# Batch 0 by halves of the heads, banks 4 and 5 as one tile, and batch 2's first matmul plain, in a fused cosformer attention and MLP kernel

## The chip, the cores and the metric

The kernel runs on one core of one Trainium2 chip. The metric is the time of one execution in microseconds (us) as the device takes it; times given as a median are over several executions of the same program. A profile comes from one execution of its own, which has its own time.

## The reference

The input is q, k and v of shape (8 batches, 8 heads, 576 positions, 64 features) and two weights, w_in (512 x 2048) and w_out (2048 x 512), all float32. First a linear attention with cosine weights, then an MLP with a squared ReLU:

```python
def phi(x, c, s):
    r = np.maximum(x, 0.0)
    return np.concatenate([r * c, r * s], axis=-1)
q_p, k_p = phi(q, cos_w, sin_w), phi(k, cos_w, sin_w)
kv = np.einsum('bhsf,bhsd->bhfd', k_p, v)
z = np.sum(k_p, axis=2)
num = np.einsum('bhsf,bhfd->bhsd', q_p, kv)
den = np.einsum('bhsf,bhf->bhs', q_p, z)[..., None] + 1e-06
x = (num / den).transpose(0, 2, 1, 3).reshape(4608, 512)
r = np.maximum(x @ w_in, 0.0)
out = (r * r) @ w_out
```

Each of the 4,608 tokens (8 batches of 576) is a row of x with 8 heads of 64 features.

## The kernel before, in words

**Tiles.** A batch's 576 positions are four tiles of 128 (called j = 0 to 3) and a tail of 64 rows; the tails of two batches share one tile. The MLP takes the 512 main tokens of batch b as group m = b, and the eight tails, 512 tokens together, as a ninth group m = 8. TensorE works on bf16 copies.

**Attention of a batch.** ScalarE (ACT) and VectorE (DVE) make the features of k and q, 128 x 512 at a time: relu times cosine and relu times sine (`feat`, L341 on ACT, L345 on DVE). v is cast into `vext`, which has a column of ones beside each head (L363, L365; for batch 0 by halves of the heads, `first_v`, L398), so that the product kv also yields z. TensorE makes kv for each head (`att_kv`, L387; batch 0: `first_kv`, L412, into bank 4 for heads 0 to 3 and bank 5 for heads 4 to 7), and a copy takes it to SBUF (`att_kvz`, L458; `first_kvz`, L423). q's features are transposed on TensorE in batches 0 and 1 (L480, copy L488), by DMA in the later ones. `att_num` (L499; `first_num`, L430) makes numerator and denominator, `att_div` (L517, L520, L523; `first_div`, L442, L443, L445) the reciprocal and the division on DVE. x is transposed (L545, copy L549; later by DMA) into xT for the MLP.

**First matmul of the MLP (x @ w_in, relu, square).** In batch 0 it runs in steps `first_mm(s, a, ...)` (L712), each on four of the sixteen hidden blocks of 128 columns and half of the tokens (256), with `first_relu` on ACT (L722) and `first_square` on DVE (L731); s goes through FIRST_S, eight steps. In batch 1 it is plain: `unit_mm` (L584) has four matmuls of 512 columns per hidden block (the first three blocks by halves, `unit_half`, L568), then a relu on ACT (L593) and squares on DVE (L601). From batch FIRST_7 = 2 on it is a scheme with seven products of half-sized blocks instead of eight (`plan_gemm1_7`; `in_product`, L661, 256 columns each), which has 112 matmuls of 256 columns per group in place of 64 of 512, but sums of x (L643), of w_in (L619, four sums, once), copies between banks on ACT (L1060, L1077), additions (L684) and maxima (L693) on DVE besides.

**Second matmul (g @ w_out).** Batch 0: `first_out` (L737) into banks 4, 5, 0, 1, with copies L770. Batch 1: plain, `out_pair` (L751) into banks 4 and 5, with copies L761. Later groups: seven products again (`plan_gemm2`; `product`, L850), with X = bank 4 and Y = bank 5 as accumulators, sums of w_out and of g on DVE (L810, L829), a copy between the banks on ACT (L1142), a copy of the fifth product's result to SBUF (L1165), and the results read by ACT (L1152) or added on DVE (L1148) into ysb, from which SP stores them (L776). In the last group (m = 8) other banks are used and the stores are split over queues: `put_part` (L784) and `put_quarter` (L792).

**PSUM.** Six banks of 128 x 512 float32, each a tile of its own (bank 0 to 5), and abank, a tile of two banks, for kv and num of the attention.

**Loads.** SP issues k, k's tail, q's tiles 0 and 1, v's first half, v's tail, v's second half and q's tiles 2 and 3 of batch 0, and later most loads and stores. POOL's queue carries w_in in four quarters, then q of batch 1 (L218), a quarter of w_out (L301), k and its tail, a quarter, v and its tail of batch 1, and two quarters. A small POOL copy ahead of these (`gate`) reads batch 0's v, first half, and so holds them until it has landed.

**What sets the order.** All of it, from the warm-up matmuls of TensorE (38 on zeros, L369) to the last store, is written down as operations with an engine (or a choice of ACT and DVE), an assumed duration, the keys they read and write, and due times; the table SHIFTS moves the due time of single operations, by their number. `Plan.order` starts, engine by engine, the ready operation that is due first, and the operations are then issued in the order of these planned starts. On the chip each engine takes its instructions strictly in that order and waits by semaphores for the tiles that it touches. Planned times (`given` for the landing of loads, `pool` for POOL's queue, `hold` for the loads of batch 2) only affect the order. The waits are made by tile: two accesses to the same tile are ordered if they may overlap.

The function that writes the list, in its part for batch 0's first matmul:

```python
for a in range(2):
    to = 2 * (n % 2) + a
    add("PE", 8 * 0.1092 * step / W, lambda a=a, c0=c0: first_mm(s, a, c0, step),
        r=[("xT", 0, j) for j in js] + [("w1", hq)], w=[("bank", to)], due=...)
```

Of the kernel before, what the change touches and what calls it, by code (L numbers as in the profile page):

```python
# [158 lines left out]
def kernel(  # L159
# [330 lines left out]
    NUM = [abank[:, 0, :], abank[:, 1, :]]  # L490

    def att_num(b, j, num=NUM):
# [13 lines left out]

    def att_div(b, j, num=NUM):
        n = 2
        if num is NUM:
            parts = [(0, n, abank[:, 0:n, 0 : HH * E1])]  # L510
        else:
            parts = [(i, i + 1, num[i][:, 0 : HH * E1].unsqueeze(1)) for i in range(n)]
        parts = [(a, z, t.rearrange("p b (h e) -> p b h e", e=E1)) for a, z, t in parts]
        den = odd.tile([P, 2, HH], F32, name="den", tag="den", bufs=2)
        rden = odd.tile([P, 2, HH], F32, name="rden", tag="rden", bufs=2)
        for a, z, n4 in parts:
            nc.vector.tensor_single_scalar(  # L517
                out=den[:, a:z], in_=n4[:, :, :, D], scalar=EPS, op=ALU.add
            )
        nc.vector.reciprocal(out=rden[:, 0:n], in_=den[:, 0:n])  # L520
        x = x_of(b, j).rearrange("p (b k) (l d) -> p b k l d", b=n, l=2)
        for a, z, n4 in parts:
            nc.vector.tensor_tensor(  # L523
                out=x[:, a:z],
                in0=n4[:, :, :, 0:D].rearrange("p b (k l) d -> p b k l d", l=2),
                in1=rden[:, a:z]
                .rearrange("p b (k l) -> p b k l", l=2)
                .unsqueeze(4)
                .to_broadcast([P, z - a, HH // 2, 2, D]),
                op=ALU.mult,  # L530
            )
# [10 lines left out]
    def att_x_pe(b, j, to):  # L542
        dst = as_bf16(bank[to][:, :], KB)
        for kb in range(KB):
            nc.tensor.transpose(dst[:, kb, :], x_of(b, j)[:, kb, :], ident[:, :])  # L545

# [157 lines left out]
    FIRST_S = (0, 4, 1, 5, 2, 6, 3, 7)  # L704

    def first_mm(s, a, c0, step):
        half, hq = s // 4, s % 4
        for c in (c0,):
            for i in (2 * a, 2 * a + 1):
                hb = hq * 4 + i  # L710
                for kb in range(KB):
                    nc.tensor.matmul(  # L712
                        out=bank[2 * (FIRST_S.index(s) % 2) + i // 2][:, i % 2 * W + c : i % 2 * W + c + step],
                        lhsT=w1sb[:, kb, hb * P : (hb + 1) * P],
                        rhs=xT_of(0)[:, half, kb, c : c + step],
                        start=(kb == 0),
                        stop=(kb == KB - 1),
                    )
# [229 lines left out]
    def plan_qT(b, i):  # L948
# [3 lines left out]
        for j in js:  # L952
            where[b, j] = ("qpT", i)
# [4 lines left out]
    def plan_qT_pe(b, j, to, due, eng):  # L958
# [3 lines left out]
        add(eng, cost(eng, 1024, "psum") if eng == "ACT" else 0.60, lambda: att_qT_copy(b, j, 0, H, to, ENG[eng]),  # L962
            r=[("bank", to)], w=[("qpTp", slot)])
        where[b, j] = ("qpTp", slot)
# [4 lines left out]
    def plan_num(b, j, due):  # L969
        r = [where[b, j], ("kvz", b % 3)] + ([("kvz", (b + 1) % 3)] if j == J else [])  # L970
        add("PE", 0.27 if j < J else 0.36, lambda: att_num(b, j), r=r, w=[("T",)], due=due)
# [489 lines left out]
```

## Time and profile before

| what | value |
|---|---|
| median of three runs | 275.63 us (275.6 to 275.7) |
| the profiled execution | 276.42 us |
| its span (first to last instruction) | 274.6 us |
| granted clock of TensorE, mean | 0.996 |
| TensorE (PE) busy | 265.0 us, 96% |
| VectorE (DVE) busy | 225.9 us, 82% |
| ScalarE (ACT) busy | 186.8 us, 68% |
| GpSimd (POOL) busy | 15.2 us, 6% |
| read from HBM, written | 36.70 MB, 9.44 MB |
| costliest lines on TensorE | L661 (first matmul by seven products), L850 (second) |

The page of the profile gives busy times by engine (PEld is the loading of weights, beside PE), and groups of equal instructions by line, "out<-in" by the program's names, with the idle time of the engine just before them and what ended it. The chain of waits starts at the last instruction and goes back, at each step, to what released it, or to the instruction before it on its engine; "PE bank L661" is work of TensorE on line 661, "DMA k<-in_k_dram" a load, "issue" time without a wait that the profile shows. The windows give busy times for stretches of the span; a DMA share above 1 means that the packets' times overlap on the 16 DMA engines. Lines of the timeline are runs of one instruction, with start, length, and in brackets the idle time before them and what ended it. SPq, ACTq and POOLq are the engines' issue of DMAs.

### The profile page before, as it was taken

The page shows a single profiled execution, that of the slowest core. Times are in us where ns is not written, and L with a number is a line of the kernel's source. Part 1 is how long each engine was busy: PE and PEld are TensorE (multiplying, and loading weights), DVE is VectorE, ACT ScalarE, POOL GpSimd, SP SyncE. Part 2 cuts the span into 40 slices and gives each one's busy share as a digit, 9 for nine tenths or more (in the row PEclk, how much of TensorE's full clock was granted, in tenths as well). Part 3 has the DMA queues.
Part 4 walks back from the last instruction along what each step waited for, and adds up shares of the span by engine and source line. Part 5 has one row for each costly group of instructions (what it writes and reads, how often), then busy time and mean ns, then how long its engine had stood idle before and what let it go on. Part 6 is the DMA issues. An engine that isn't in the chain of part 4 may idle for free.

```text
span 274.6 us, 6700 instructions
## 1 busy us (share of the span) xinstructions
PE 265.0 (96%) x2698; PEld 215.2 (78%) x2706; DVE 225.9 (82%) x450; ACT 186.8 (68%) x336; POOL 15.2 (6%) x29
## 2 busy tenths in 40 slices
PE   8989999999999999999999999999999999999993
PEld 3669856565478669899998889989988888888882
DVE  1865997947969999999999999999989974888911
ACT  3865671696689899898879997865646763464231
POOL 1563100000000000000000000000000000000022
PEclk9999999999999999999999999999999999999998
DMA  7999999999998979999999999985202100300134
GB/s 213 306 204 276 284 279 284 296 245 297 264 289 255 259 202 282 329 246 168 287 301 241 230 271 253 165 183 181 41 1 96 79 2 0 155 1 2 76 117 115
DMA packets 87006, 53.38 MB, mean 194 GB/s; under 512 B 56928, under 2 KB 83936, under 8 KB 86976
## 3 DMA queue, kind: packets, MB, share of 16 engines
q1 hardware_dynamic: 81504, 44.64, 63.4%
q0 software_dynamic: 5392, 8.26, 13.9%
q8 instruction: 21, 0.34, 0.5%
q10 hardware_dynamic: 80, 0.07, 0.1%
q14 instruction: 9, 0.07, 0.1%
HBM read 36.70 MB, written 9.44 MB: 168 GB/s over the span
## 4 chain that ended last, share of the span: by engine, by line
PE 80%; DMA 8%; DVE 3%; SPq 2%; issue 1%; ACT 1%; POOL 1%; POOLq 0%; DVEq 0%
PE bank L661 31%; PE bank L850 31%; DMA k<-in_k_dram 6%; PE bank L751 4%; PE bank L737 3%; PE abank L387 3%; PE bank L584 3%; PE abank L499 3%; DMA q<-in_q_dram 2%; DVE qp L345 1%; SPq L239 1%; ACT kp L341 1%; PE bank L568 1%; DVE gT L601 1%; SPq L249 1%
## 5 line engine op out<-in xcount | busy, mean ns | idle before, releaser
L661 PEld LDWEIGHTS <-w1sb 128*128 128x128 bf16 x448 | 43.3, 98 | 6.0
L661 PE MATMUL bank<-xT,w1sb 128*128 128x256 bf16 x336 | 47.8, 273 | 0.0
L850 PEld LDWEIGHTS <-gT 128*128 128x128 bf16 x448 | 43.3, 98 | 5.6 <-issue 0.6
L677 ACT ACTIVATE gT<-bank 128x512 bf16<-128x512 f32 x56 | 33.1, 600 | 16.9 <-PE bank L661 15.6
L850 PE MATMUL bank<-w2sb,gT 128*128 128x256 bf16 x336 | 41.9, 273 | 0.6 <-ACT ysb L761 0.6
L684 DVE TENSOR_TENSOR gT<-bank,qpTp 128x512 bf16<-128x512 f32 x56 | 36.7, 686 | 4.7 <-PE bank L661 3.7
L601 DVE TENSOR_TENSOR gT<-gT 128x2048 bf16<-128x2048 bf16 (+1 forms) x32 | 37.7, 1189 | 1.8 <-ACT gT L677 1.5
L1060 ACT COPY bank<-bank 128x512 f32<-128x512 f32 x56 | 31.4, 581 | 7.5 <-PE bank L661 7.0
L850 PEld LDWEIGHTS <-gs 128*128 128x128 bf16 x336 | 32.5, 98 | 3.8
L661 PEld LDWEIGHTS <-w1t 128*128 128x128 bf16 x336 | 31.9, 98 | 4.4
L661 PE MATMUL bank<-qpTp,w1t 128*128 128x256 bf16 x224 | 32.7, 273 | 0.0
L850 PE MATMUL bank<-w2t,gs 128*128 128x256 bf16 x224 | 27.6, 273 | 0.0
L1077 ACT COPY qpTp<-bank 128x512 f32<-128x512 f32 x28 | 16.1, 589 | 9.8 <-PE bank L661 5.6
L523 DVE TENSOR_TENSOR x<-abank,rden 128x512 bf16<-128x512 f32 x30 | 20.7, 691 | 1.0
L1148 DVE TENSOR_TENSOR ysb<-bank,y 128x512 f32<-128x512 f32 x14 | 9.7, 690 | 9.6 <-PE bank L850 8.3
L661 PE MATMUL bank<-xT,w1t 128*128 128x256 bf16 x112 | 16.8, 272 | 0.0
L661 PE MATMUL bank<-zeros,w1sb 128*128 128x256 bf16 x112 | 16.6, 273 | 0.0
L712 PE MATMUL bank<-xT,w1sb 128*128 128x256 bf16 (+1 forms) x160 | 15.5, 251 | 0.6 <-ACT gT L722 0.6
L341 ACT ACTIVATE qp<-q,sin_col 128x512 bf16<-128x512 f32 x23 | 16.1, 717 | 0.0
L784 POOL DMA_DIRECT2D out_dram<-ysb x4 | 2.4, 613 | 237.6 <-ACT ysb L1152 235.2
L341 ACT ACTIVATE kp<-k,cos_col 128x512 bf16<-128x512 f32 x18 | 12.6, 715 | 4.3 <-DMA k<-in_k_dram 4.3
L751 PE MATMUL bank<-w2sb,gT 128*128 128x512 bf16 x60 | 14.9, 379 | 0.5 <-DVE gT L601 0.3
(118 smaller groups left out, 423.5 us busy)
## 6 DMA issues: line engine op xcount, KB each, us to landing
out_dram<-ysb SPq DMA_DIRECT2D x16, 512.0 KB, 3.9
q<-in_q_dram SPq DMA_DIRECT2D x14, 512.0 KB, 6.3
v<-in_v_dram SPq DMA_DIRECT2D x14, 512.0 KB, 6.0
k<-in_k_dram SPq DMA_DIRECT2D x12, 512.0 KB, 6.7
w1sb<-in_moe_w_in_dram POOLq DMA_DIRECT2D x4, 512.0 KB, 9.3
w2sb<-in_moe_w_out_dram POOLq DMA_DIRECT2D x4, 512.0 KB, 17.5
k<-in_k_dram SPq DMA_DIRECT2D x1, 1024.0 KB, 5.6
q<-in_q_dram POOLq DMA_DIRECT2D x1, 1024.0 KB, 11.9
```

The lines of the kernel that those rows point to most:

```text
L341: eng.activation(out=dst[ps, :, lo : lo + D], in_=src[ps], func=ACTF.Relu, scale=col[ps])
L523: nc.vector.tensor_tensor(out=x[:, a:z], in0=n4[:, :, :, 0:D].rearrange("p b (k l) d -> p b k l d", l=2), in1=rden[:, a:z] .rearrange("p b ...
L601: nc.vector.tensor_tensor(out=g, in0=g, in1=g, op=ALU.mult)
L661: nc.tensor.matmul(out=bank[to][:, s * W : (s + 1) * W], lhsT=lhs[:, kb, (2 * u + s) * P : (2 * u + s + 1) * P], rhs=rhs[:, kb, :], start= ...
L677: nc.scalar.activation(out=g_pair(m, i, j, u), in_=bank[to][:, :].rearrange("p (s c) -> p s c", s=2), func=ACTF.Relu,)
L684: nc.vector.tensor_tensor(out=g_pair(m, i, j, u), in0=bank[to][:, :].rearrange("p (s c) -> p s c", s=2), in1=in_five(u).rearrange("p (s c) ...
L712: nc.tensor.matmul(out=bank[2 * (FIRST_S.index(s) % 2) + i // 2][:, i % 2 * W + c : i % 2 * W + c + step], lhsT=w1sb[:, kb, hb * P : (hb + ...
L751: nc.tensor.matmul(out=bank[LAST_Y[s_]][:, :], lhsT=gT_of(m)[:, hb, tt * P : (tt + 1) * P], rhs=w2sb[:, hb, :], start=(hb == 0), stop=(hb ...
L850: nc.tensor.matmul(out=bank[to][:, s * DM2 : (s + 1) * DM2], lhsT=lhs[:, hb, s * P : (s + 1) * P], rhs=rhs[:, hb, :], start=(fresh and hb ...
L1060: add("ACT", psum, lambda: nc.scalar.copy(out=bank[b][:, :], in_=bank[a][:, :]), r=[("bank", a)], w=[("bank", b)])
L1077: add("ACT", psum, lambda u=u, Y=Y: nc.scalar.copy(out=in_five(u), in_=bank[Y][:, :]), r=[("bank", Y)], w=five)
L1148: lambda: nc.vector.tensor_tensor(out=y_view(m, i, cc), in0=half_bank(a), in1=five_of(m)[:, :, :], op=ALU.add),
```

## The change

- **PSUM.** Banks 4 and 5 become the halves of one tile of two banks, `bbank`; "bank 6" is a name for abank's first half.
- **Batch 0's loads.** k's and v's tails are issued by ScalarE's queue, ahead of its own table load and activations; SP keeps k, q's tiles 0 and 1, v's halves, q's tiles 2 and 3, in this order. The gate on POOL reads v's tail instead of v's first half.
- **Batch 0's attention.** The copies of q's transposes go by halves of the heads (`att_qT_part`), on whichever of ACT and DVE is planned first; x of tiles 0 and 1 is transposed and copied by halves of the heads, all into bank 4 (`first_x_pe`, `first_x_copy`); kv takes tiles (0, 1), (2, 3) and the tail as separate steps. Both q transposes of tiles 2 and 3 use bank 5. num of tile 3 is written to bbank, and x's transposes of tiles 2 and 3 to bank 6 and bank 4.
- **Batch 0's first matmul.** Step s = 0 is split once more, by halves of the inner dimension (`kbs`), each needing only the x of one half of the heads. FIRST_S keeps four steps (hidden blocks 0 to 7); blocks 8 to 15 become plain units of 512 columns (`unit_mm`) with squares by four blocks.
- **Batch 2.** FIRST_7 goes from 2 to 3: batch 2's first matmul is plain, its sums, additions, maxima and copies between banks go, and the four sums of w_in move to batch 3.
- **att_div** loses its form for separate banks. The planned times of loads and the holds of batch 2's loads change, and SHIFTS is replaced by a new table throughout (cut here).

```diff
-    bank = [psum.tile([P, FP], F32, name=f"bank{i}") for i in range(6)]
+    bank = [psum.tile([P, FP], F32, name=f"bank{i}") for i in range(4)]
+    bbank = psum.tile([P, 2, FP], F32, name="bbank")
     abank = psum.tile([P, 2, FP], F32, name="abank")
+    bank += [bbank[:, 0, :], bbank[:, 1, :], abank[:, 0, :]]
...
-        nc.gpsimd.tensor_copy(out=got[:, :], in_=kqv["v", 0][:, 0, 0, 0:1])
+        nc.gpsimd.tensor_copy(out=got[rows(0), :], in_=kqv["vt", 0][rows(0), 0, 0:1])
...
+    def att_qT_part(b, j, h0, h1, to, eng):
...
+        copy(out=qpTs[b, j, "t"][:, h0:h1, :], in_=as_bf16(bank[to][:, :], H)[:, h0:h1, :])
...
+    def first_x_pe(j, half, to):
+        dst = as_bf16(bank[to][:, :], 2 * KB)
+        for kb in (2 * half, 2 * half + 1):
+            nc.tensor.transpose(dst[:, KB * j + kb, :], x_of(0, j)[:, kb, :], ident[:, :])
+
+    def first_x_copy(j, half, to, eng):
+        copy = eng.copy if eng is nc.scalar else eng.tensor_copy
+        kbs = slice(2 * half, 2 * half + 2)
+        copy(
+            out=xT_of(0)[:, j // 2, kbs, j % 2 * P : (j % 2 + 1) * P],
+            in_=as_bf16(bank[to][:, :], 2 * KB)[:, KB * j + 2 * half : KB * j + 2 * half + 2, :],
+        )
...
-    FIRST_S = (0, 4, 1, 5, 2, 6, 3, 7)
-
-    def first_mm(s, a, c0, step):
+    FIRST_S = (0, 4, 1, 5)
+
+    def first_mm(s, a, c, step, kbs=range(4)):
...
+        for k0 in range(2 if s == 0 else 1):
+            kbs = (2 * k0, 2 * k0 + 1) if s == 0 else range(KB)
+            for c0, step in parts:
...
         for js, r in (
-            (range(J), [("v0", half, i) for i in range(2)] + [("kp", j, x) for j in range(J) for x in "cs"]),
+            ((0, 1), [("v0", half, 0)] + [("kp", j, x) for j in (0, 1) for x in "cs"]),
+            ((2, 3), [("v0", half, 1)] + [("kp", j, x) for j in (2, 3) for x in "cs"]),
             ((J,), [("kpt", 0, "c"), ("kpt", 0, "s"), ("vt", 0, 0)]),
         ):
...
-        plan_num(0, j, TM + 0.5 + 0.8 * (j - 2))
-        plan_x_pe(0, j, 4 + j % 2, TM + 1.8 + 0.8 * (j - 2), "DVE")
+        keys = [("T",), ("bank", 4), ("bank", 5)][j - 2 :][: j - 1]
+        plan_num(0, j, TM + 0.5 + 0.8 * (j - 2), (abank, bbank)[j - 2], keys)
+        plan_x_pe(0, j, (6, 4)[j - 2], TM + 1.8 + 0.8 * (j - 2), None, keys)
...
+    for hb in range(4 * len(FIRST_S) // 2, HB):
+        n = hb - 4 * len(FIRST_S) // 2
+        plan_unit(0, hb, n % 4, TM + len(FIRST_S) * dt0 + n * dt0 / 2)
...
-    FIRST_7, STRIDE, SHIFT = 2, 2.0, -6.0
+    FIRST_7, STRIDE, SHIFT = 3, 2.0, -6.0
...
-            hold = {"v": 41.0, "k": 43.0, "q": 43.1}[nm] if b == 2 else 0.0
+            hold = {"v": 40.0, "k": 41.5, "q": 41.6}[nm] if b == 2 else 0.0
...
         load_main("k", 0, nc.sync)
-        load_tail("k", 0, nc.sync)
+        load_tail("k", 0, nc.scalar)
+        load_tail("v", 0, nc.scalar)
         load_tiles("q", 0, nc.sync, slice(0, 2))
         load_half("v", 0, nc.sync, 0)
-        load_tail("v", 0, nc.sync)
         load_half("v", 0, nc.sync, 1)
         load_tiles("q", 0, nc.sync, slice(2, 4))
```

More of the change, by code (lines that the diff above doesn't have):

```diff
@@ L505, in att_num, with att_div @@
                     )
[L507 to L513, printed above, removed]
+    def att_div(b, j, to=abank):
+        n4 = to[:, :, 0 : HH * E1].rearrange("p b (h e) -> p b h e", e=E1)
         den = odd.tile([P, 2, HH], F32, name="den", tag="den", bufs=2)
         rden = odd.tile([P, 2, HH], F32, name="rden", tag="rden", bufs=2)
[L516 to L531, printed above, removed]
+        nc.vector.tensor_single_scalar(out=den[:, :], in_=n4[:, :, :, D], scalar=EPS, op=ALU.add)
+        nc.vector.reciprocal(out=rden[:, :], in_=den[:, :])
+        x = x_of(b, j).rearrange("p (b k) (l d) -> p b k l d", b=2, l=2)
+        nc.vector.tensor_tensor(
+            out=x[:, :],
+            in0=n4[:, :, :, 0:D].rearrange("p b (k l) d -> p b k l d", l=2),
+            in1=rden[:, :]
+            .rearrange("p b (k l) -> p b k l", l=2)
+            .unsqueeze(4)
+            .to_broadcast([P, 2, HH // 2, 2, D]),
+            op=ALU.mult,
+        )
     def att_x(b, i):
@@ L701, in in_max @@
         nc.vector.tensor_single_scalar(out=g, in_=g, scalar=0.0, op=ALU.max)
-    FIRST_S = (0, 4, 1, 5, 2, 6, 3, 7)
-    def first_mm(s, a, c0, step):
+    FIRST_S = (0, 4, 1, 5)
+    def first_mm(s, a, c, step, kbs=range(4)):
         half, hq = s // 4, s % 4
[L708 to L718, printed above, removed]
+        for i in range(2):
+            hb = hq * 4 + 2 * a + i
+            for kb in kbs:
+                nc.tensor.matmul(
+                    out=bank[2 * (FIRST_S.index(s) % 2) + a][:, i * W + c : i * W + c + step],
+                    lhsT=w1sb[:, kb, hb * P : (hb + 1) * P],
+                    rhs=xT_of(0)[:, half, kb, c : c + step],
+                    start=(kb == 0 and i == 0 and c == 0),
+                    stop=(kb == KB - 1),
+                    skip_group_check=True,
+                )
     def first_relu(s, a):
@@ L961, in plan_qT_pe, with plan_num @@
         add("PE", 8 * 0.057, lambda: att_qT_pe(b, j, 0, H, to), r=q_parts((j,)), w=[("bank", to)], due=due)
-        add(eng, cost(eng, 1024, "psum") if eng == "ACT" else 0.60, lambda: att_qT_copy(b, j, 0, H, to, ENG[eng]),
-            r=[("bank", to)], w=[("qpTp", slot)])
-        where[b, j] = ("qpTp", slot)
+        if b == 0:
+            for h in (0, HH):
+                add(EITHER, (0.33, 0.48), lambda e, h=h: att_qT_part(b, j, h, h + HH, to, ENG[e]),
+                    r=[("bank", to)], w=[("qpTp", slot, h)])
+            where[b, j] = [("qpTp", slot, 0), ("qpTp", slot, HH)]
+        else:
+            add(eng, cost(eng, 1024, "psum") if eng == "ACT" else 0.60, lambda: att_qT_copy(b, j, 0, H, to, ENG[eng]),
+                r=[("bank", to)], w=[("qpTp", slot), ("qpTp", slot, 0), ("qpTp", slot, HH)])
+            where[b, j] = [("qpTp", slot)]
     def x_key(j):
         return ("xt",) if j == J else ("x", j)
-    def plan_num(b, j, due):
-        r = [where[b, j], ("kvz", b % 3)] + ([("kvz", (b + 1) % 3)] if j == J else [])
-        add("PE", 0.27 if j < J else 0.36, lambda: att_num(b, j), r=r, w=[("T",)], due=due)
-        add("DVE", 1.05, lambda: att_div(b, j), r=[("T",)], w=[x_key(j)])
+    def plan_num(b, j, due, to=abank, keys=(("T",),)):
+        r = where[b, j] + [("kvz", b % 3)] + ([("kvz", (b + 1) % 3)] if j == J else [])
+        add("PE", 0.27 if j < J else 0.36, lambda: att_num(b, j, to), r=r, w=keys, due=due)
+        add("DVE", 1.05, lambda: att_div(b, j, to), r=keys, w=[x_key(j)])
     def plan_x(b, i):
@@ L980, in plan_x, with plan_x_pe @@
             add("SP", 1.4, lambda: att_x(b, i), r=[x_key(j) for j in js], w=w, lag=1.7 + CARE)
-    def plan_x_pe(b, j, to, due, eng):
-        add("PE", 4 * 0.057, lambda: att_x_pe(b, j, to), r=[x_key(j)], w=[("bank", to)], due=due)
-        add(eng, cost(eng, 512, "psum") if eng == "ACT" else 0.34, lambda: att_x_copy(b, j, to, ENG[eng]),
-            r=[("bank", to)], w=[("xT", b % 2, j)])
+    def plan_x_pe(b, j, to, due, eng, keys=None):
+        keys = keys or [("bank", to)]
+        add("PE", 4 * 0.057, lambda: att_x_pe(b, j, to), r=[x_key(j)], w=keys, due=due)
+        engs = (eng,) if eng else EITHER
+        add(engs, tuple(cost(e, 512, "psum") if e == "ACT" else 0.34 for e in engs), lambda e: att_x_copy(b, j, to, ENG[e]),
+            r=keys, w=[("xT", b % 2, j)])
     def plan_unit(m, hb, to, due, halves=False):
@@ L1287 @@
         add("PE", 0.216, lambda: warm(1), w=[("T",)], due=20.0, after=9.2 + 0.5 * i)
-    add("POOL", 0.1, gate, r=[("v", 0)], due=0.0)
-    plan_pool(2.6, lambda: load_w1(0, 4), [("w1", 0)])
-    for i in range(1, 4):
-        plan_pool(2.6, lambda i=i: load_w1(i, 4), [("w1", i)])
     for j in range(NS):
@@ L1296 @@
         plan_qT_pe(0, j, j, 10.0 + 0.3 * j, "DVE" if j == 0 else "ACT")
+    add("POOL", 0.1, gate, r=[("vt", 0)], due=0.0)
+    for i, at in enumerate((15.8, 18.9, 21.5, 24.1)):
+        plan_pool(at, lambda i=i: load_w1(i, 4), [("w1", i)])
     for half in range(2):
-        for i, e in enumerate(("DVE", "ACT")):
+        for i in range(2):
             js = slice(2 * i, 2 * i + 2)
-            add(e, cost(e, FP, "cast"), lambda half=half, js=js, e=e: first_v(half, js, ENG[e]),
-                r=[("v", half)], w=[("v0", half, i)])
+            add_either(FP, "cast", lambda e, half=half, js=js: first_v(half, js, e), [("v", half)], [("v0", half, i)])
         if half == 0:
@@ L1312 @@
         for half in range(2):
-            add("PE", 0.14, lambda j=j, half=half: first_num(j, half), r=[where[0, j], ("kvz", 0, half)],
+            add("PE", 0.14, lambda j=j, half=half: first_num(j, half), r=[where[0, j][half], ("kvz", 0, half)],
                 w=[("bank", 2 * j + half)], due=12.5 + 0.3 * j)
-            add("DVE", 0.65, lambda j=j, half=half: first_div(j, half), r=[("bank", 2 * j + half)], w=[("x", j)])
-        plan_x_pe(0, j, 4 + j, TM - 0.5 + 0.9 * j, "ACT")
+            add("DVE", 0.72, lambda j=j, half=half: first_div(j, half), r=[("bank", 2 * j + half)], w=[("x0", j, half)])
@@ L1317 @@
+        for half in range(2):
+            add("PE", 2 * 0.057, lambda j=j, half=half: first_x_pe(j, half, 4), r=[("x0", j, half), ("kvz", 0, 0)],
+                w=[("x4", j, half)], due=TM - 1.0 + 0.7 * half + 0.4 * j)
+            add(EITHER, (0.20, 0.30), lambda e, j=j, half=half: first_x_copy(j, half, 4, ENG[e]),
+                r=[("x4", j, half)], w=[("xT0", j, half)])
     for j in (2, 3):
         plan_q(0, j, src=[("q23",)])
-        plan_qT_pe(0, j, 4 + j % 2, TM - 1.0 + 0.4 * (j - 2), "DVE" if j == 2 else "ACT")
+        plan_qT_pe(0, j, 5, TM - 1.0 + 0.4 * (j - 2), None)
@@ L1320 @@
     for i in range(2):
         add("PE", 0.0, lambda: None, r=[("kvz", 0, i)], w=[("kvz", 0)])
+    for j in range(2):
+        add("PE", 0.0, lambda: None, r=[("x0", j, 0), ("x0", j, 1)], w=[("x", j)])
+        add("PE", 0.0, lambda: None, r=[("xT0", j, 0), ("xT0", j, 1)], w=[("xT", 0, j)])
+    add("PE", 0.0, lambda: None, r=[("xT", 0, 0), ("xT", 0, 1)], w=[("bank", 4)])
     for j in (2, 3):
-        plan_num(0, j, TM + 0.5 + 0.8 * (j - 2))
-        plan_x_pe(0, j, 4 + j % 2, TM + 1.8 + 0.8 * (j - 2), "DVE")
@@ L1335 @@
+    plan_pool(32.8, lambda: load_tail("k", 1, nc.gpsimd), [("kt", 1)])
+    plan_pool(35.0, lambda: load_w2(1, 4), [("w2", 1)])
+    plan_pool(38.1, lambda: load_main("v", 1, nc.gpsimd), [("v", 0), ("v", 1)])
+    plan_pool(38.5, lambda: load_tail("v", 1, nc.gpsimd), [("vt", 1)])
+    for i, at in ((2, 40.8), (3, 43.4)):
+        plan_pool(at, lambda i=i: load_w2(i, 4), [("w2", i)])
     for s in FIRST_S:
         plan_first(s)
+    for hb in range(4 * len(FIRST_S) // 2, HB):
+        n = hb - 4 * len(FIRST_S) // 2
+        plan_unit(0, hb, n % 4, TM + len(FIRST_S) * dt0 + n * dt0 / 2)
+        if n % 4 == 3:
+            add("DVE", 0.06 + 2048 * 0.00053, lambda u=hb // 4: square(0, u, True),
+                w=[key for x in range(hb - 3, hb + 1) for i in range(2) for key in g_keys(0, i, x // HB2, (x % HB2,))])
```

48 lines of the change are left out of this document (23 added, 25 removed), and 85 rows, old and new, of the table SHIFTS.

## The prediction, made before the changed kernel was run

> **What bounds the kernel now.** The median of three runs is 275.63 us; the profiled execution took 276.42 (span 274.6, 1.8 outside it). I sum differences in the profiled execution and add them to the median; 0.2% is 0.55 us, about the least that a measurement of this kernel can tell from no change.
>
> I read first the page's shares and the engine line of the chain of waits:
>
> ```profile
> PE 265.0 (96%) x2698; PEld 215.2 (78%) x2706; DVE 225.9 (82%) x450; ACT 186.8 (68%) x336; POOL 15.2 (6%) x29
> PE 80%; DMA 8%; DVE 3%; SPq 2%; issue 1%; ACT 1%; POOL 1%; POOLq 0%; DVEq 0%
> ```
>
> TensorE is the bound, so its work counts one for one wherever it has no idle time. A busy PE may still be a stretched one, so I took the windows by stage (core 0; columns: elapsed, then PE, PEld, DVE, ACT, POOL busy, granted clock, DMA share, GB/s), cut at batch 0's first MLP matmul, near the landing of batch 1's k, at batch 1's first MLP matmul (L568), inside batch 2's stage, after the last idle time of PE, and at the end of its steady work:
>
> ```profile
> 17.67:33.76 16.09, 16.07 (x211) 14.95 (x209) 11.90 (x23) 10.20 (x18) 5.19 (x7) 1.00 1.15 266
> 33.76:52.97 19.21, 18.39 (x167) 10.73 (x168) 16.58 (x36) 9.33 (x16) 0.00 (x0) 1.00 1.10 303
> 52.97:71.42 18.45, 18.07 (x158) 10.51 (x157) 13.31 (x31) 15.59 (x29) 0.00 (x0) 1.00 1.09 260
> 71.42:101.12 29.70, 28.62 (x278) 19.86 (x280) 26.83 (x56) 24.80 (x46) 0.00 (x0) 1.00 0.99 252
> 101.12:269.06 167.94, 167.94 (x1762) 150.43 (x1762) 147.57 (x275) 115.42 (x211) 2.43 (x4) 1.00 0.63 154
> ```
>
> To see: from 101.12 on PE has no idle time at all. Between 52.97 and 101.12, 1.9 us are missing by work at full rate (below). Ahead of 42 us the DMA share is above 1: transfers, not engines, are scarce there. The chain shows what that does (start, length, what):
>
> ```profile
> 17.36 16.59 DMA k<-in_k_dram
> 33.98 2.56 ACT kp L341 x4
> 36.54 0.49 ACT gT L722
> 37.07 1.03 PE bank L712 x8
> ```
>
> Prices of TensorE from runs of equal matmuls in the chain and the timeline: eight of 512 columns 1.73 us (0.216 each), sixteen of 256 1.75 (0.109), eight transposes 0.45 (0.056), eight of 65 columns 0.245 (0.031). I counted columns in both instruction orders: 605,824 before, 609,920 after.
>
> **A. Batch 2's first matmul plain (+1.6).** 64 matmuls of 512 columns in place of 112 of 256: 64 x 0.216 = 13.84 against 112 x 0.109 = 12.25 us. It lies where TensorE is the bound. The whole difference of 4,096 columns is this one; batch 0's split steps only change shapes, and both orders have 106,640 columns ahead of batch 1's first matmul (L568).
>
> **B. Batch 0's start (-0.1; -0.9 to +1.0).** The edits: transposes, copies and the first step by halves; tails of k and v on ScalarE's queue; the gate on v's tail; wider units for blocks 8 to 15. Divisions stay four of 0.74 us each in a row, now with one half-wide copy between them. Against an earlier start: two q features stand before the first division instead of one, and they wait for the last q tiles:
>
> ```profile
> 13.22 0.77 DVE L345 TENSOR_SCALAR qp<-q,sin_col 128x512 bf16<-128x512 f32 x1 [0.37 <-DMA q<-in_q_dram]
> 13.92 0.14 DVE L442 TENSOR_SCALAR den<-bank 128x4 f32<-128x4 f32 x1
> ```
>
> So the divisions come 0.4 to 0.7 later, and finer steps (a half product needs two transposes and one copy instead of four and one wide copy) win about 1.0 back: an estimate from these rows, net some 0.5 earlier. L722's wait of 0.56 at 36.5 (relu queued on ScalarE behind four features that wait for batch 1's k) goes too, since the relus now stand before those features. But what is late next is batch 1's v:
>
> ```profile
> 40.07 1.66 ACT L363 CAST vext<-v 128x512 bf16<-128x512 f32 x3 [1.33 <-DMA v<-in_v_dram]
> 40.98 1.20 PE L387 MATMUL abank<-vext,kp 128*128 128x65 bf16 x32
> ```
>
> Before, PE came to L387 at 40.98 just as it could start. After, 1,024 columns (0.43) fewer stand ahead of it, and with the gains above PE is there at 39.7 to 40.2. v lands at 40.0, 19.6 us after its issue, queued behind w1, q, w2 and k; the gate opens within some tenths of where it did and the DMA engines have no slack, so I let v land when it did. L387 then starts near 40.6 (0.4 earlier: the landing and 0.62 for the first cast), with the 0.43 of work behind it instead of ahead: nothing won. Of the stage's idle 0.9, 0.3 is left beside the L712 wait; halved, it makes -0.15, so I take -0.1. The bounds: PE's arrival gets all of it (-0.9), or the divisions' lateness is passed on in full (0.7) with one more wait of 0.3 (+1.0).
>
> At this place the DMA engines' sharing decides. Rows: SP's issues of the two tails take 0.74 us (from 1.26) and 1.21 (from 4.98); ScalarE would spend 1.95 on them, ahead of a table load of 1.28 and two small activations, done near 4.5, where its first feature waits until 6.44: hidden. The Trainium skill (DMA: Bandwidth & Descriptors, "Issuing engines are not separate DMA queues") says that transfers issued by several engines share the same 16 DMA engines and interleave, and that a second issuer saves only issue time. The trace agrees as far as it goes: 331 to 345 GB/s from 4 to 12 us, with one issuer. By that rule the last loads land when they did; were the issue time the limit, they would land 0.7 earlier, and the rival of an early v is what that would feed.
>
> **C. Idle time between 52.97 and 101.12 (-1.1; -1.9 to +0.5).** Found in the timeline:
>
> ```profile
> 53.90 1.47 PE L568 MATMUL bank<-xT,w1sb 128*128 128x256 bf16 x12 [0.33 <-DVE ysb L770]
> ...
> 101.12 1.91 PE L850 MATMUL bank<-w2sb,gT 128*128 128x256 bf16 x16 [0.64 <-ACT ysb L761]
> ```
>
> The first waits for a DVE copy of batch 0's output (4 narrow and 4 wide matmuls, 1.3 us, stand in between after), the second for a ScalarE copy queued behind features (eight matmuls, 0.87, stand in between after). A third, 0.29 at 74.48, waits for squares on DVE; batch 2 loses 4 sums, 8 additions and 4 maxima there (8 additions at 0.69 alone are 5.5 us), but three or four sums of w1 (1.14 to 1.22 each) move from about 30 to 40 and 70 us into this stretch. I keep 0.8 of the 1.9: -1.1. All of it may go (-1.9), or the sums add waits (+0.5: one sum of 1.2 less the 0.7 between a DVE read's start and what needs it).
>
> The simpler att_div issues the same instructions for batches 1 to 8, and the holds of batch 2's loads (40 to 41.6 for 41 to 43.1) only rank them: their buffers come free with batch 1's features and casts, after 40.07. Both at nothing.
>
> **D. The end (+0.35; 0 to +0.9).** In the new order the product that makes y5, which both last DVE additions read, comes second to last, so the addition for the first half ends some 0.6 later against PE's end; SP issues its third store 1.0 instead of 0.45 behind PE (270.37 before), and POOL puts four stores out in another order. I take about 0.35 of the 0.55 for the last landing, since landings of 2.4 to 3.0 us overlap.
>
> **E. One tile for two banks (+0.95; 0 to +2.5).** Banks 4 and 5 become halves of one tile, bbank; the built order then has TensorE, before it writes one half, wait for the last read of the other half. They are also the pair of the later batches' second matmul (L850), whose results DVE and ACT read. Behind a waiting matmul all of PE stands. The trace of before has no such wait (no idle time on PE). Its readers are prompt (out<-in xcount | busy, mean ns | idle before, releaser), and the last one shows how late a read ends:
>
> ```profile
> L1148 DVE TENSOR_TENSOR ysb<-bank,y 128x512 f32<-128x512 f32 x14 | 9.7, 690 | 9.6 <-PE bank L850 8.3
> ```
> ```profile
> 268.01 1.91 PE L850 MATMUL bank<-w2t,gT 128*128 128x256 bf16 x16
> 268.21 0.69 DVE L1148 TENSOR_TENSOR ysb<-bank,y 128x512 f32<-128x512 f32 x1 [1.00 <-PE bank L850]
> ```
>
> A read ends 0.2 + 0.69 = 0.89 after the last matmul on DVE (268.90; the next product begins at 268.01), 0.2 + 0.585 = 0.79 on ACT (L1152). I counted 15 such waits from the first L850 on, with the PE work between the bank's last write and the waiting matmul: 0.44 us twice (ACT), 0.68 once (DVE), 0.87 seven times, 1.31 or more five times. The stall is the difference: 2 x 0.35 + 0.2 + a few hundredths for the DVE ones of 0.87, with what a semaphore adds, about 0.95. Bounds: nothing, if the order's slack hides them all; +2.5, if ten readers stand 0.15 behind other work as well.
>
> **Sum.** 1.6 - 0.1 - 1.1 + 0.35 + 0.95 = +1.7; D and E overlap in the last batch, where I take 0.2 off: +1.5, 277.1 us, slower by 0.5%. SHIFTS is replaced throughout, so the order elsewhere is new too; since PE idles nowhere there, this can only add, and I price it within the range (+-0.3).
>
> **Rivals.**
> R1, no difference: all idle time of C goes and the readers are early enough for E to cost 0.3. 1.6 - 0.1 - 1.9 + 0.35 + 0.3 = +0.25: 275.9. For it: 1.9 us are there to be had, and DVE loses some 8 us of work. Against: the readers' 0.89 is longer than 0.44 in any order.
> R2, faster (the other side): batch 1's v lands early. It decides from where v lands before 39.4: then PE meets no wait at 39.9, and B is -0.9 to -1.0. With R1's C and the low sides of D and E: 1.6 - 0.95 - 1.9 + 0.2 + 0.05 = -1.0: 274.6. For it: the batch's k and q loads stand ahead of v on POOL's queue, and a gate opened earlier moves all of them. Against: a DMA share above 1 throughout.
> R3, heavier waits: readers of the pair stand behind other work on DVE or ACT, so 13 to 15 waits of up to 0.6 come, some 4 us less the slack: with E at +3.0 and the rest as forecast, +3.5: 279.1. For it: DVE is 82% busy over the span. Against: the readers start at once in before.
> R4, the change doesn't do what it says: the first matmul starts later, as two features stand ahead of the first division, and by over 1 us, so that v's wait no longer covers it: B +0.9, +2.5: 278.1.
>
> **How the numbers follow.** Forecast 0.43 (277.1; own range 276.2 to 278.2), R1 0.17, R2 0.24, R3 0.09, R4 0.07. Slower by over 0.2% is the forecast, R3 and R4, less 0.02 for the forecast's low edge: 0.57; within 0.2% R1 and that edge: 0.19; faster: 0.24. Cases of both signs hold chance, so the range goes from R2's time less 0.2 (274.4) to 278.6, halfway into R3; it leaves out part of R2 and most of R3, under 2 in 10.
>
> **What would show it.** A: batch 2 by L603 (L584 before) in place of L680 (L661), and 1.6 us more PE busy. B: the start of L394 (L387) and what it waits for (v's cast; if it starts at PE's own pace before 40, R2). C: idle of PE between 53 and 101, under 1 us. D: from the last matmul's end to the span's end 5.0 us or more (269.92 to 274.60 before, 4.68). E: idle on first matmuls of L869 (L850 before) with ACT or DVE copies as the releaser, two of some 0.35; none at all means the tile costs nothing. Wrong would be PE idle under 0.3 in all after 53 us (R1, R2), or v landed before 39.4 (R2).

## The result, and the profile after

The changed kernel takes 289.0 us (median of 6 runs, 288.86 to 289.25) against 275.63 (median of 6, 275.39 to 276.02): a ratio of 1.0484, 95% interval 1.0471 to 1.0498. That is 13.4 us slower, where 1.5 were forecast, and far outside the range. Its profiled execution has a span of 287.2 us, 12.6 more than that of before, whose profiled execution took 0.8 us more than its median.

The page of the changed kernel, its engine line and the engine line of the chain:

```profile
PE 267.9 (93%) x2619; PEld 207.3 (72%) x2626; DVE 219.9 (77%) x443; ACT 181.9 (63%) x327; POOL 15.4 (5%) x29
PE 73%; DVE 9%; ACT 8%; issue 5%; DMA 2%; POOL 1%; POOLq 0%; ACTq 0%; DVEq 0%
```

TensorE's share of the chain fell from 80% to 73%, and DVE and ACT, 4% together before, have 17%: the end now hangs on their work as well. The windows by the stages of before (same columns) say where:

```profile
17.67:33.76 16.09, 13.87 (x168) 11.13 (x168) 9.85 (x25) 10.00 (x18) 4.71 (x7) 1.00 1.16 271
33.76:52.97 19.21, 18.95 (x166) 10.56 (x166) 14.20 (x31) 7.76 (x13) 0.00 (x0) 1.00 1.11 307
52.97:71.42 18.45, 18.40 (x162) 10.80 (x161) 14.34 (x34) 14.43 (x26) 0.00 (x0) 1.00 0.78 178
71.42:101.12 29.70, 29.60 (x212) 14.66 (x213) 23.53 (x44) 19.96 (x35) 0.00 (x0) 1.00 1.02 276
101.12:269.06 167.94, 162.81 (x1707) 143.69 (x1706) 147.75 (x280) 115.91 (x210) 0.00 (x0) 1.00 0.58 152
```

Two stretches lose: the start (13.87 busy of 16.09, where it was 16.07) and the long steady part, which had no idle time on TensorE at all and now has 5.1. Between 53 and 101 us it is the other way round: 0.15 idle of 48.15. The waits of TensorE on this trace (engine, line, waited for: us in total, times, longest) name the cause by the tile:

```profile
PE bbank L869 <- DVE ysb L1175: 2.1, 4, 0.8
PE bbank L869 <- ACT ysb L1179: 1.7, 3, 0.7
PE bank L487 <- ACT qp L348: 1.2, 1, 1.2
PE bbank L869 <- ACT y L1192: 1.2, 2, 0.7
...
PE bbank L556 <- DVE xT L561: 0.8, 1, 0.8
PE bbank L487 <- ACT xT L561: 0.7, 1, 0.7
PE bbank L869 <- ACT bank L1230: 0.7, 1, 0.7
PE bbank L514 <- DVE xT L561: 0.7, 1, 0.7
PE bbank L869 <- ACT ysb L780: 0.7, 1, 0.7
```

But for the first transposes of batch 0 (L487, 1.2) and the start of the warm-up, every one of 0.7 or more is TensorE about to write bbank. One such place in the timeline shows that there are two waits, not one:

```profile
131.39 1.03 PE L869 MATMUL bbank<-w2sb,gs 128*128 128x256 bf16 x8 [0.24 <-ACT ysb L1179]
...
132.26 1.04 PE L869 MATMUL bbank<-w2sb,gT 128*128 128x256 bf16 x8
...
133.39 0.69 DVE L1175 TENSOR_TENSOR ysb<-bbank,y 128x512 f32<-128x512 f32 x1 [1.31 <-ACT kp L348]
...
134.13 1.03 PE L869 MATMUL bbank<-w2sb,gT 128*128 128x256 bf16 x8 [0.84 <-DVE ysb L1175]
```

The second half of product 3 (gs) fills bank 5 and ends where the next run begins, at 132.26. Its result could be read 0.2 later, as in before. But DVE reads it at 133.39, after the following run, which is the first half of the next group's product 1 into bank 4, has ended. Then TensorE, about to write the second half of that product into bank 4, waits until the read of bank 5 is done. DVE's bracket names ACT, whose features of k this addition does not need. The true releaser is the run on the other half of bbank: the addition waits for a semaphore of TensorE, and in this trace TensorE signals at 130.72 and next at 133.30, the end of the run on bank 4; at the end of product 3 there is no signal. None of the 0.87 us of TensorE's work between the bank's last write and the waiting matmul hides any of the read.

The shown idle is also short. A run of eight is recorded with 1.03 us, and runs follow each other every 0.87 without a gap (131.39 to 132.26), so each wait costs 0.16 more than its bracket.

The difference of the spans, cut at batch 1's first MLP matmul (52.97 before, 54.77 after), at the end of the work ahead of the first seven-product run of the second matmul (100.49, where the wait of L850 begins; 102.56, of L869), and at TensorE's last end (269.92; 280.64): +1.80, +0.27, +8.65, and +1.88 behind TensorE's end (4.68; 6.56): 12.6 in all.

### The profile page after: what moved, and what is told of

Read it like the earlier page. It is cut to its first block, busy times and chain, and to the rows that moved or that the text cites. A ratio compares the mean times of both kernels' runs of the same rounds, so it can differ in the third digit from the quotient of the medians.

```text
span 287.2 us, 6490 instructions
## 1 busy us (share of the span) xinstructions
PE 267.9 (93%) x2619; PEld 207.3 (72%) x2626; DVE 219.9 (77%) x443; ACT 181.9 (63%) x327; POOL 15.4 (5%) x29
## 4 chain that ended last, share of the span: by engine, by line
PE 73%; DVE 9%; ACT 8%; issue 5%; DMA 2%; POOL 1%; POOLq 0%; ACTq 0%; DVEq 0%
PE bank L680 22%; PE bbank L869 22%; PE bank L603 9%; PE bbank L770 3%; PE abank L394 3%; PE bank L869 3%; PE bank L756 2%; PE bbank L756 2%; PE bank L730 2%; PE abank L514 2%; DMA k<-in_k_dram 2%; DVE gT L620 2%; ACT qp L348 2%; ACT kp L348 1%; DVE ysb L1175 1%
## 5 line engine op out<-in xcount | busy, mean ns | idle before, releaser
L869 PEld LDWEIGHTS <-gT 128*128 128x128 bf16 x448 | 43.4, 98 | 9.9 <-issue 4.7
L869 PE MATMUL bbank<-w2sb,gT 128*128 128x256 bf16 x304 | 38.6, 272 | 3.7 <-DVE ysb L1175 1.7
L680 PE MATMUL bank<-xT,w1sb 128*128 128x256 bf16 x288 | 41.4, 273 | 0.0
L696 ACT ACTIVATE gT<-bank 128x512 bf16<-128x512 f32 x48 | 28.3, 598 | 18.8 <-PE bank L680 18.5
L680 PEld LDWEIGHTS <-w1sb 128*128 128x128 bf16 x384 | 36.9, 98 | 4.4
L869 PEld LDWEIGHTS <-gs 128*128 128x128 bf16 x336 | 32.5, 98 | 8.0 <-issue 4.3
L703 DVE TENSOR_TENSOR gT<-bank,qpTp 128x512 bf16<-128x512 f32 x48 | 31.0, 684 | 8.8 <-PE bank L680 8.5
L603 PE MATMUL bank<-xT,w1sb 128*128 128x512 bf16 x148 | 34.9, 379 | 0.0
L612 ACT ACTIVATE gT<-bank 128x512 bf16<-128x512 f32 x40 | 23.4, 600 | 17.1 <-PE bank L603 16.9
L869 PE MATMUL bbank<-w2t,gs 128*128 128x256 bf16 x208 | 26.1, 272 | 2.3 <-ACT bank L1230 0.7
L680 PE MATMUL bank<-qpTp,w1t 128*128 128x256 bf16 x192 | 28.1, 273 | 0.0
L603 PEld LDWEIGHTS <-w1sb 128*128 128x128 bf16 x148 | 13.6, 98 | 14.1
L1104 ACT COPY qpTp<-bank 128x512 f32<-128x512 f32 x24 | 13.8, 590 | 13.4 <-PE bank L680 12.8
L348 ACT ACTIVATE qp<-q,cos_col 128x512 bf16<-128x512 f32 x21 | 14.7, 715 | 0.2 <-DMA q<-in_q_dram 0.2
L770 PE MATMUL bbank<-w2sb,gT 128*128 128x512 bf16 x61 | 14.3, 379 | 0.2
```

Of the source, the lines that this page charges most:

```text
L348: eng.activation(out=dst[ps, :, lo : lo + D], in_=src[ps], func=ACTF.Relu, scale=col[ps])
L603: nc.tensor.matmul(out=out_, lhsT=w1sb[:, kb, hb * P : (hb + 1) * P], rhs=x_block(m, kb), start=(kb == 0), stop=(kb == KB - 1),)
L612: nc.scalar.activation(out=gT_of(m)[:, hb, :], in_=bank[to][:, :], func=ACTF.Relu)
L680: nc.tensor.matmul(out=bank[to][:, s * W : (s + 1) * W], lhsT=lhs[:, kb, (2 * u + s) * P : (2 * u + s + 1) * P], rhs=rhs[:, kb, :], start= ...
L696: nc.scalar.activation(out=g_pair(m, i, j, u), in_=bank[to][:, :].rearrange("p (s c) -> p s c", s=2), func=ACTF.Relu,)
L703: nc.vector.tensor_tensor(out=g_pair(m, i, j, u), in0=bank[to][:, :].rearrange("p (s c) -> p s c", s=2), in1=in_five(u).rearrange("p (s c) ...
```

## The experiments

Ratios are to the kernel before, run beside each kernel on the same chip, with a 95% interval. Numbers are medians.

**Two tiles again (e1_split).** The edit, with the division of batch 0's j = 3 done by two tiles:

```diff
-    bank = [psum.tile([P, FP], F32, name=f"bank{i}") for i in range(4)]
-    bbank = psum.tile([P, 2, FP], F32, name="bbank")
+    bank = [psum.tile([P, FP], F32, name=f"bank{i}") for i in range(6)]
     abank = psum.tile([P, 2, FP], F32, name="abank")
-    bank += [bbank[:, 0, :], bbank[:, 1, :], abank[:, 0, :]]
+    bbank = bank[4:6]
+    bank += [abank[:, 0, :]]
```

> The changed kernel with banks 4 and 5 as two tiles again (batch 0's num of j = 3 reads and writes them as two tiles, so one division becomes two operations of half the width plus one more small one); the order of operations is kept. Theory T (one tile makes every read of one half wait for the last write of the other half that stands ahead of it in the order, and then TensorE wait for that read): the idle time on L869 (6.6 us shown, 13 places) is gone and each place gives back some 0.16 us more that a restart costs; the waits of 0.5 to 0.8 between 16 and 33 us partly stay, as batch 0's x copies still share bank 4. Time 289.0 - 8.7 - 1 to 2 = 278 to 279.5, and the wait at the end of the span stays. Rival R (the readers are late in this order, whatever the tiles): idle on L869 stays above 4 us and the time stays above 285.

Measured: 278.04, ratio 1.0087 (1.0054 to 1.012), 11.0 us less than the changed kernel. All the waits of TensorE for another engine that its trace has after the warm-up's start:

```profile
PE bank L514 <- DVE xT L567: 0.6, 1, 0.6
PE bank L562 <- DVE xT L567: 0.4, 1, 0.4
PE bank L487 <- ACT qp L348: 0.3, 1, 0.3
```

What this list leaves out is under 0.1: on the products, 0.06 and 0.03. Nearly nothing waits for a product's reader any more. Between batch 1's first MLP matmul and the first product both kernels take the same time to the hundredth (47.79 us: 52.31 to 100.10, and 54.77 to 102.56); the whole 11.0 lies ahead of it (2.46) and behind it up to TensorE's end (169.55 against 178.08 us: 8.53). The tail behind TensorE's end is the same (6.55, 6.56). Of the 8.53, about 6.5 is idle that the changed kernel's trace shows, at 13 places, and the rest makes 0.16 a place. The order of the work is unchanged but for the one division, so the rival, readers late by the order, falls.

**The tile alone, in the kernel before (e2_before_pair).**

```diff
-    bank = [psum.tile([P, FP], F32, name=f"bank{i}") for i in range(6)]
+    bank = [psum.tile([P, FP], F32, name=f"bank{i}") for i in range(4)]
+    bbank = psum.tile([P, 2, FP], F32, name="bbank")
+    bank += [bbank[:, 0, :], bbank[:, 1, :]]
```

> The kernel before with one edit: banks 4 and 5 are the halves of one tile. Theory T: TensorE gets idle time on L850, at 10 to 20 places with a reader on DVE or ACT as the releaser and 0.2 to 0.85 us each, each with about 0.16 of restart: 6 to 12 us slower, 282 to 288. Rival R (only the new order makes the readers late): within 1 us of 275.6.

Measured: 283.72, ratio 1.029 (1.0262 to 1.0318): 8.0 us for one declaration, in the order of before. The waits of TensorE that lead its list:

```profile
PE bbank L852 <- ACT ysb L1154: 2.1, 5, 0.7
...
PE bbank L482 <- DVE qpTp L490: 1.0, 1, 1.0
PE bbank L852 <- DVE ysb L763: 0.8, 1, 0.8
```

Before had none of these. With e1_split this shows that the shared tile is the cause, in either order.

**Seven products for batch 2 again (e3_split_seven).** From e1_split, FIRST_7 back to 2; the shifts keep to their operations, and some were moved.

```diff
-    FIRST_7, STRIDE, SHIFT = 3, 2.0, -6.0
+    FIRST_7, STRIDE, SHIFT = 2, 2.0, -6.0
```

> e1_split with batch 2's first matmul by seven products again (FIRST_7 = 2); the shifts follow their operations to the new numbers, and some are moved so that the written order has no idle time planned. Theory (A is pure work of TensorE, 1.6 us, wherever the order is tight): TensorE's busy time falls by about 1.6, idle on it between 50 and 105 us stays under 0.5, and the time is 278.0 - 1.6 = 276.4, more or less by up to 1 us for other last stores. Rival (plain batch 2 is what removed the idle time of C): over 1.0 us of idle comes back between 50 and 105 us, and the time stays at 277.4 or above.

Measured: 276.68, ratio 1.0034 (1.0018 to 1.005), 1.4 us under e1_split. TensorE's busy time falls from 266.5 to 265.0 us, but it ends at the same time, 269.64 against 269.65. Idle comes back in place of the work, 1.1 us in all between 50 and 105 us (the longest 0.66, for a DMA transpose of x, and 0.30, for a copy between banks) and 0.35 at 266.9, as the rival has it. What is gained in the trace lies behind TensorE's end: the span ends 5.0 us after it instead of 6.6, with the last stores in a better order. So the 1.4 does not measure A.

**Plain batch 2 alone (e4_before_plain).** The kernel before with FIRST_7 = 3.

> The kernel before with batch 2's first matmul plain (FIRST_7 = 3) and nothing else of the change; shifts follow their operations, some moved as in e3. Theory: 1.6 us of work are added and at most the 1.3 us of idle time between 53 and 101 us can be won back: 275.9 to 277.3. Rival (the planned relief of DVE is worth more than its work on TensorE): below 275.2.

Measured: 278.39, ratio 1.0092 (1.0056 to 1.0128). PE is busy 2.0 us more than before, and idle between 50 and 101 us falls from 1.3 to 0.16 us, as the forecast's C had it. It is slower than expected for a reason of its order: 1.67 us at 34.66, a matmul waits for a relu that stands on ScalarE behind features of batch 1's k. So A's price and C's gain are seen, and their sum is not cleanly measured here.

**The late stores by other queues (e5_last_queue).**

```diff
-        store_half(1, 1, ("POOL", "POOL"))
+        store_half(1, 1, ("ACT", "SP"))
```

> e1_split with the two stores of the last group that POOL issues last (the half that the second y5 addition makes) issued by ScalarE and SP instead. Theory (the late end is POOL's issue of these stores behind its two quarter stores, 270.59 and 271.2, with landing at 276.2): the last landing comes 1.2 to 1.9 earlier, 276.1 to 276.9. Rival (the landing of any store takes until then, since they share the transfer engines): within 0.4 of 278.0.

Measured: 277.47, ratio 1.0066 (1.0049 to 1.0084). The stretch behind TensorE's end is 6.13 us, 0.42 less than in e1_split: the stores of the late addition now leave ACT and SP, the last of them SP at 271.19. It lands at 274.55, no earlier than POOL's last store in e1_split (274.64): 5.08 and 4.99 us behind TensorE's end. What is shorter is the rest, from the last landing to the end of the span: 1.08 instead of 1.60. So the forecast of an earlier landing fails, and the time alone can't tell the two kernels apart (the intervals overlap).

**Batch 0's loads as before, in e1_split (e6_old_loads).** Both tails on SP, the gate on v's first half.

> e1_split with batch 0's loads as before (both tails on SP in their old places, the gate on v's first half); order of all other work kept. Theory (tails on ScalarE's queue let the loads behind them and the gate go earlier, and so batch 1's v lands at 38.7 instead of 40.0): v lands at 39.4 or later, batch 1's kv step starts at 40.3 to 40.9 instead of 39.94, and the time is 278.4 to 278.9. Rival (the earlier landing comes from the order of operations, whose buffers free batch 1's loads earlier): v lands within 0.3 of 38.7 and the time stays within 0.2 of 278.0.

Measured: 278.61, ratio 1.0092 (1.0059 to 1.0125), not to be told from e1_split by the intervals. v lands at 39.06, in between. Its trace ends later (TensorE at 271.09 instead of 269.65) for another reason: the first transposes of q wait 1.69 us (0.30 in e1_split) for a DVE feature, and in this order the cast of v's tail, which lands later with the old loads, stands ahead of that feature on DVE. So the order and the loads of the change belong together; the question of v's landing is not decided.

**The y5 additions early (e7_tail).** e1_split with shifts of the last 25 us moved, so that products 5, 7, 3 come ahead of the second half of 2.

> e1_split with the shifts of operations in the last 25 us changed, so that in the written order the last group's products 5 and 7 come ahead of 3, 4 and 2, and both y5 additions are done three to four us before TensorE's end; all else as e1_split. Theory (the late end of e1_split, 6.55 us behind TensorE's end where it was 4.68 before, comes from product 5 standing second to last, so that the second addition ends after TensorE and its stores come last on POOL): the last POOL store is issued at about 270.1 instead of 271.2, the span ends 0.9 to 1.8 us earlier, and the time is 276.2 to 277.1. Rival (the landing of the last stores sets the end, whichever they are): within 0.3 of 278.0.

Measured: 277.17, ratio 1.005 (1.0033 to 1.0067). The additions start at 264.58 and 266.27, and the span ends 5.77 us behind TensorE instead of 6.55 (4.68 in before). About 0.8 of the 1.9 is thus the additions' lateness. The last issues on POOL in e1_split, then in e7_tail:

```profile
270.59 1.22 POOL L809 DMA_DIRECT2D out_dram<-ysb  x2
```
```profile
269.76 1.21 POOL L815 DMA_DIRECT2D out_dram<-ysb  x2 [0.89 <-ACT ysb L1191]
```

Both are half stores (128 KB each). The second of each pair lands at 274.64 and 273.88, 3.45 and 3.5 us after its issue begins, and the span ends 1.6 us after that landing in both. In before the last issues are quarter stores (64 KB) on SP and ACT; the last lands at 273.37, and the span ends 1.27 after it. In e7_tail the very last landing is that of ACT's quarter store (274.05, 3.9 after its issue; 3.0 in before), 4.33 us behind TensorE's end where before has 3.45. Why it takes longer is not separated here.

**The loads alone, in the kernel before (e8_new_loads).**

```diff
-        load_tail("k", 0, nc.sync)
+        load_tail("k", 0, nc.scalar)
+        load_tail("v", 0, nc.scalar)
         load_tiles("q", 0, nc.sync, slice(0, 2))
         load_half("v", 0, nc.sync, 0)
-        load_tail("v", 0, nc.sync)
```

> The kernel before with one part of the change: both tails of batch 0 on ScalarE's queue ahead of its table load, SP's order k, q01, v, v, q23, and the gate on v's tail; the order of all else as before. Theory (the 16 transfer engines are the limit between 4 and 12 us, and a second issuer saves only issue time): q23 lands within 0.3 us of 13.2, batch 0's first MLP matmul starts within 0.3 of 17.67, and the time is within 0.4 of 275.6. Rival (SP's issue is the limit): q23 lands 0.6 or more earlier and the time is 275.1 or less, as far as batch 1's v allows.

Measured: 275.67, ratio 0.9995 (0.997 to 1.0021): no difference. The start shows why (k landed, q23 landed, first MLP matmul):

```profile
6.94 0.72 ACT L341 ACTIVATE kp<-k,cos_col 128x512 bf16<-128x512 f32 x1 [3.02 <-DMA k<-in_k_dram]
...
13.14 0.72 ACT L341 ACTIVATE qp<-q,cos_col 128x512 bf16<-128x512 f32 x1 [0.48 <-DMA q<-in_q_dram]
...
17.65 0.61 PE L712 MATMUL bank<-xT,w1sb 128*128 128x128 bf16 x8
```

k lands 0.5 later than before (6.44), as it does with the old loads in e6_old_loads (7.02), q23 0.08 earlier, and the first matmul starts at 17.65 instead of 17.67. In this trace batch 1's v landed at 38.41, and its first MLP matmul started 0.82 us earlier than before (52.15); at 177.2 us TensorE then waits 0.56 for a DMA transpose of x, which it does not in before, and its end is 269.84 (269.92). A gain at the start was given back.

**A version meant to beat both (e9_seven_again).** e3_split_seven with its shifts searched again.

> e3_split_seven (separate tiles, seven products for batch 2, the change's start and loads) with a written order that was searched again, with 1.2 us more allowed for DMA transposes and the late stores weighed in. Theory (what is good in the change is its earlier start by 0.7 us; what is bad is the shared tile, the plain batch 2 and the late stores): with idle under 0.5 us on TensorE after 50 us it takes 274.8 to 275.6, at or a little under the kernel before. Rival (the start's gain is always given back at a later wait, as on a DMA transpose in e8_new_loads and e3_split_seven): idle of 0.5 or more on a DMA transpose or a copy comes in its place and the time is 275.8 to 276.7.

Measured: 285.12 (median of six, 283.35 to 288.39, the widest spread here), ratio 1.0326 (1.0284 to 1.0368). Both theories miss. The new order has waits that its assumed durations did not foresee: 2.14 us at 34.64 behind a relu on ScalarE, 1.87 at 102.29 for a DMA transpose, and smaller ones; TensorE ends at 277.16, 7.5 us behind e3_split_seven's. Of these, 4.0 are there at batch 1's first MLP matmul (56.02; 52.04): the wait of 2.14, and then a lower clock, which the page shows in its sixth slice (7.05 us each, in tenths of full speed):

```profile
PEclk9999979999999999999999999999999999999998
```

The granted clock is 0.5 from 37.59 to 41.00 us, and a run of sixteen matmuls of 512 columns takes 5.30 us there, where two runs of eight (1.90 each as recorded, at 43.78 and 45.76) make 3.6: some 1.7 us. The other ten traces have the full clock from 7.1 us to TensorE's end. The drop follows the wait; that the wait brought it on is not shown (after the 1.67 us in e4_before_plain there is none). The later idle, 3.8 us against 1.5 in e3_split_seven, explains most of the remaining 3.5. No version here beats the kernel before.

## Why the prediction was wrong, step by step

**E failed.** It was put at +0.95 and measured 11.0 (e1_split). The cause was named rightly, "TensorE, before it writes one half, wait for the last read of the other half", and the places were nearly right (15 counted, 13 found). The two halves never overlap, and accesses to them are ordered all the same, as e2_before_pair shows. What was missed is the other side of the same rule: the read, too, waits for the last write of the other half that stands ahead of it. The working priced the stall as the read's end (0.89 or 0.79 after "the last matmul") less TensorE's work since "the bank's last write". With both waits the clock of the read starts at the end of that very work, so nothing is subtracted: a place whose 0.87 us of work was to hide nearly all of the read, as the one at 134.13, costs 0.84 as shown, and 0.16 more for the restart that the brackets leave out. R3 had more stalls in it, but for another reason (readers behind other work) and at 3.0, too little; e2_before_pair shows that no late order is needed.

The count also began at the first L850. The start was left out, where the shared tile costs 2.46 us (e1_split), since batch 0 uses both halves for kv, transposes and num at once. **B**, forecast at -0.1, came out at +1.8 with the tile and at -0.66 without it (52.31 in e1_split). That last is R2's side, as v landed at 38.7, before the 39.4 that the prediction named as the sign; but e8_new_loads reaches 52.15 without any of the splitting by halves, so the splitting is not shown to win anything. R4 did not come: batch 0's first MLP matmul started earlier, at 16.78 (16.22 in e1_split, 17.67 before). To "let v land when it did" was wrong by over a us. Its first cast starts at 37.8 to 38.8 in the seven traces with the new loads, and at 38.8 to 40.1 in the four with the old ones (40.07 in before is the latest). It goes with the gate: w1's first issue on POOL is at 9.1 to 10.3 in the seven traces with the new loads (earliest in e7_tail, where v's cast is the earliest too), and at 9.90 in e4_before_plain (v at 38.77), where before, e2_before_pair and e6_old_loads have 10.58 to 10.73 (v at 39.1 to 40.1). That the gate is the cause is argued from these rows; no run moved the gate by itself.

At the same place the Trainium skill (DMA: Bandwidth & Descriptors, "Issuing engines are not separate DMA queues") held: a second issuer brought neither the last loads nor the first matmul forward by as much as 0.1 us (e8_new_loads: 13.14 and 17.65; 13.22 and 17.67 before).

**A** was right: the forecast's 1.6 is the difference in TensorE's busy time between batch 1's first MLP matmul and TensorE's end, of before (215.5) and e1_split (217.1). e3_split_seven takes 1.5 of busy time back, though not of TensorE's end. **C** was right in kind and nearly in size: all of the 1.3 us that the trace of before shows idle there is gone, and 1.1 was forecast; e4_before_plain shows that plain batch 2 alone does it. **D** named the late addition rightly and had a fifth of the size: 0.35 where 1.87 came. The last landing is 1.54 later behind TensorE's end than in before (4.99; 3.45), and the span ends 1.60 instead of 1.27 after it. Of the 1.87, 0.8 goes with the late additions (e7_tail); the other 1.1 is not separated. The forecast took landings of 2.4 to 3.0 that overlap; the last three stores of e1_split take 3.2 to 3.6 us from issue to landing.

The sum without E: 1.6 - 0.66 - 1.33 + 1.87 = 1.5 us, against 1.6 of span in e1_split (2.3 between the medians). The forecast's four terms without E make 0.75; they erred by -0.56 in B, -0.23 in C and +1.52 in D.

## What to carry to other kernels

If two accumulators become one tile in this framework, a read of one half waits for every write to the other half that stands ahead of it in the order, and the next write to either half waits for that read, so neither overlaps the other. Price such a wait from the end of the last write to the tile, not to the half, and count them from the first use of the tile. A bracket that names an engine with nothing to give, as ACT at 133.39, is the sign to look for what ended just before.

## What was not expected of the hardware

A store's landing is not the end. In the six traces in which POOL issues a half store last (e1_split among them), the span ended 1.6 us after that store had landed; it was 1.27 after ACT's quarter store in before, and 1.08 after SP's half store in e5_last_queue. From issue to landing POOL's last half store (3.45 us in e1_split) and SP's (3.36 in e5_last_queue) took about the same. An idle bracket on TensorE understates a stall by 0.16 us, since a run's recorded end (1.03 us for eight matmuls) is later than the next run can follow (0.87). And a stall can be followed by a lower clock, as in e9_seven_again: 0.5 for 3.4 us.
